# Decode holds, tiny steps on GpSimd and a later bias in a fused attention and two-expert-layer kernel

## The chip, the cores and the metric

The kernel runs on one core of one Trainium2 chip, as one launch. The metric is the device time of that launch in microseconds (us); lower is better. The core has TensorE (PE in the profile, its weight loads PEld), VectorE (DVE), ScalarE (ACT), GpSimd (POOL) and SyncE (SP), each with an instruction queue of its own that it works off in order, and DMA queues. TensorE's clock has two levels here, 1.2 and 2.4 GHz; the profile gives it as 0.5 and 1.0 of full speed.

## The reference

Three layers, all in float32, on 2304 tokens (4 sequences of 576) of width 512:

```python
scores = scale * q @ k^T, a causal window of 64, softmax        # 8 heads of 64
x = attention @ v                                               # 2304 x 512
h = x @ w_in;  g = softplus(h);  x = g @ w_out                  # 512 -> 2048 -> 512
logits = x @ w_gate + modality_bias[modality_id]                # 8 experts
out = p_best * (relu(x @ w1[e]) @ w2[e]),  e = argmax(logits)   # 512 -> 1024 -> 512
```

## The kernel before, in words

The kernel works in float32 accuracy out of reduced-precision matmuls: every matrix is split into a high part and the rest, and three matmuls (high by high, high by rest, rest by high) make one product.

The tokens of the first two layers are cut into 6 blocks of 384. Attention goes in chunks of 64 queries (c = 0 to 35, six to a block): `a_scores` makes the scores on TensorE, takes each row's maximum on VectorE (L143), scales it by -1/8 (L144, a 128x4 tile) and takes four exponentials on ScalarE (L148), which also give the row sums; `a_norm` adds 1e-9 to the sums (L153, 128x4), inverts them (L154) and multiplies (L159 on VectorE for the first block, L157 on ScalarE for the second, L159 on GpSimd from the third on); `a_probs` transposes the probabilities on TensorE (L165) and copies them out of PSUM on ScalarE (L167, tile pT); `a_av` multiplies by v (L180) and splits the result into xh (ScalarE, L181) and xl (VectorE, L88 called from L182). A block of the next layer can begin once xh and xl of its six chunks are there. "First-block attention" below means chunks 0 to 5, which run at the start; chunks 6 to 11 run beside the first block of the second layer, spread over its steps by `attn_slots`.

The second layer is 16 steps f of 128 hidden columns for each block b: `mm1(b, f)` is 12 matmuls (L238 to L240) into a PSUM tile ph, of which there are two, then softplus on ScalarE and VectorE (the "gate": L245, L246, L250 and L254 on ScalarE, L251 and the difference gl of L255 on VectorE; from the second block on L248 takes L245's place and gl is made on GpSimd); `mm2(b, f)`, two steps later, is 9 matmuls (L267 to L269).

The weights of step f, both of w_in and w_out, come from memory as 64-bit floats and are decoded in the kernel once, by `w_decode(f)`, during the start and the first block: ScalarE takes the absolute value (L222), VectorE does two clamping and shifting steps (L223, L224) and two merging steps (L225, L226), ScalarE rounds the high part (L227), VectorE takes the rest (L88 called from L228). For f in `HALVES` = (0, 1, 2) this goes in two halves of 512 columns, for the others in one pass of 1024. The decoded weights W0 to W15 stay on the chip, and the five later blocks use them again. The program calls `w_decode(0)` and `w_decode(1)` inside the loop over the first six chunks (L721), and `w_decode(f + 2)` in step f of the first block (L747).

`r_consts` (L305, called in step 2 of the first block) loads the small constants of the third layer and forms the bias of each token, `btok`, by five VectorE instructions (L316 to L321). `btok` is first read by `r_pick(0)`, in step 5 of the second block. The third layer starts after the sixth block with gathered tokens.

The order of an engine's instructions isn't written by hand: a planner walks the program with its own estimate of times and lets each engine take the earliest instruction of the program that it holds to be ready. So VectorE's queue can have a decode instruction ahead of an attention instruction that comes earlier in the program. `wait_for` (L202) adds a wait on another instruction, which the planner also respects. On the chip the order is then fixed.

Of the kernel before, what the change touches and what calls it, by code (L numbers as in the profile page):

```python
# [19 lines left out]
P = 128  # L20
# [14 lines left out]
def attention_moe_moe_kernel(ctx, tc, q, k, v, w_in, w_out, modality, w_gate, mod_bias, w1, w2, out):  # L35
# [17 lines left out]
    TPB = TB // P  # L53
    SCALE = 1.0 / 8.0
    LAG = 2
    HALVES = (0, 1, 2)
    BUSY = 2 * CPB
    R = N + P
    MR = 4
# [28 lines left out]
        eng.tensor_tensor(out_, a, hi.bitcast(F32), ALU.subtract)  # L88

    at = {}  # L90
    xblk = {}


# [22 lines left out]
    def a_scores(c, tags=None, s=None):  # L116
        w = at[c]
        win, n, qT, kT = w["win"], w["n"], w["q"], w["k"]
        if tags is None:
            both = ps.tile([P, 2, 4, P], F32, name="pss", tag="pS")  # L120
            parts = [both[:, :, 0:2, 0:n]]
            bank = [both[:, z, 0:2, 0:n] for z in range(2)]
        else:
            bank = [ps.tile([P, 2, P], F32, name=f"pss{z}", tag=tags[0], bufs=tags[1])[:, :, 0:n] for z in range(2)]
            parts = [x[:, None] for x in bank]
        for i in range(2):
            heads = [(2 * i + e, z) for e in range(2) for z in range(2)]
            outs = [bank[z][half(j, z) * C:(half(j, z) + 1) * C, i, :] for j, z in heads]
            for (j, z), o in zip(heads, outs):
                r = slice(z * C, (z + 1) * C)  # L130
                nc.tensor.matmul(o, qT[r, j, :], kT[r, :, j, :], start=True, stop=c >= BUSY)
            if c < BUSY:
                for (j, z), o in zip(heads, outs):
                    r = slice(z * C, (z + 1) * C)
                    nc.tensor.matmul(o, identb[r, r], mask[r, win], start=False, stop=True)
        s = sb.tile([P, 2, 2, P], F32, name="s") if s is None else s
        if c >= BUSY:
            nc.vector.tensor_tensor(s[:, :, :, 0:n], parts[0], mask[:, None, None, win].to_broadcast((P, 2, 2, n)), ALU.add)
            parts = [s[:, :, :, 0:n]]
            bank = [s[:, z, :, 0:n] for z in range(2)]  # L140
        mx = sb.tile([P, 2, 2], F32, name="mx")
        for i, x in enumerate(parts):
            nc.vector.tensor_reduce(out=mx[:, i:i + x.shape[1]], in_=x, axis=AX.X, op=ALU.max)  # L143
        nc.vector.tensor_scalar(mx, mx, -SCALE, None, ALU.mult)  # L144
        sm = sb.tile([P, NPR], F32, name="sm")
        for z in range(2):
            for i in range(2):
                nc.scalar.activation(s[:, z, i, 0:n], bank[z][:, i, :], AF.Exp, bias=mx[:, z, i:i + 1], scale=SCALE, accum_out=sm[:, 2 * z + i:2 * z + i + 1])  # L148
        w.update(s=s.rearrange("p z i k -> p (z i) k"), sm=sm)

    def a_norm(c):
        s, sm, n = at[c]["s"], at[c].pop("sm"), at[c]["n"]
        nc.vector.tensor_scalar(sm, sm, 1e-9, None, ALU.add)  # L153
        nc.vector.reciprocal(sm, sm)  # L154
        if CPB <= c < BUSY:
            for i in range(NPR):
                nc.scalar.activation(s[:, i, 0:n], s[:, i, 0:n], AF.Copy, scale=sm[:, i:i + 1])  # L157
        else:
            (nc.vector if c < CPB else nc.gpsimd).tensor_tensor(s[:, :, 0:n], s[:, :, 0:n], sm[:, :, None].to_broadcast((P, NPR, n)), ALU.mult)  # L159

    def a_probs(c, tag="pA", bufs=1, pT=None):
        s, n = at[c].pop("s"), at[c]["n"]
        pp = ps.tile([P, NPR, P], F32, name="pp", tag=tag, bufs=bufs)
        for j in range(NPR):
            nc.tensor.transpose(pp[0:n, j, :], s[:, j, 0:n], ident)  # L165
        pT = sb.tile([P, NPR, P], F32, name="pT", bufs=1) if pT is None else pT
        nc.scalar.copy(pT[0:n], pp[0:n])  # L167
        at[c]["pT"] = pT

    def a_av(c, tag="pA"):  # L170
# [27 lines left out]

    W = {}
    raws = {}  # L200

    def wait_for(later, earlier, reason):  # L202
        tc.add_manual_dep(later.ins, earlier.ins.name, mybir.DependencyInfo(mybir.DependencyClass.Sync, mybir.DependencyReason.DATA), reason=reason)
# [10 lines left out]
    def w_decode(f):  # L214

        raw = raws.pop(f)
        w = wp.tile([P, 2, 2, 512], F32R, name=f"W{f}", tag="W")
        t = sb.tile([P, 2, 512], I32, name="wt", bufs=1)
        for h in ([slice(0, 1), slice(1, 2)] if f in HALVES else [slice(0, 2)]):
            hw, lw, th = raw[:, h, :, 1], raw[:, h, :, 0], t[:, h, :]  # L220
            tf, hf = th.bitcast(F32), hw.bitcast(F32)
            nc.scalar.activation(tf, hf, AF.Abs)  # L222
            nc.vector.tensor_scalar(tf, tf, LEAST, MOST, ALU.max, ALU.min)  # L223
            nc.vector.tensor_scalar(th, th, 3, 0x3FFFFFF8, ALU.logical_shift_left, ALU.bitwise_and)  # L224
            nc.vector.scalar_tensor_tensor(hw, hw, SIGN_EXP, th, ALU.bitwise_and, ALU.bitwise_or)  # L225
            nc.vector.scalar_tensor_tensor(hw, lw, 29, hw, ALU.logical_shift_right, ALU.bitwise_or)  # L226
            nc.scalar.copy(w[:, h, 0, :], hf)  # L227
            diff(nc.vector, w[:, h, 1, :], hf, w[:, h, 0, :])  # L228
        W[f] = w
# [75 lines left out]
    def r_consts():  # L305
        nc.sync.dma_start(wg, w_gate.rearrange("(k p) e -> p k e", p=P))
        nc.sync.dma_start(bias2, mod_bias.rearrange("m e -> (m e)")[None, :].to_broadcast((P, 2 * E)).rearrange("p (m e) -> p m e", m=2))
        nc.sync.dma_start(mraw, modality.bitcast(I32).rearrange("(t p two) -> p t two", p=P, two=2))

        scr = wp.tile([P, 2048], F32, name="scr0", tag="W")  # L310
        tini = scr[:, :E * R // P * MR].bitcast(I32).rearrange("p (r m) -> p r m", m=MR)
        nc.gpsimd.memset(tini, 0)
        nc.gpsimd.memset(tini[:, :, 0:1], 4 * N)
        nc.sync.dma_start(meta.rearrange("(p r) m -> p r m", p=P), tini)
        sel = scr[:, 1024:1024 + 2 * NT].rearrange("p (m t) -> p m t", m=2)
        nc.vector.tensor_scalar(sel[:, 0], mraw[:, :, 0], 0.0, None, ALU.is_equal)  # L316
        nc.vector.tensor_scalar(sel[:, 1], mraw[:, :, 0], 0.0, None, ALU.not_equal)
        b1 = scr[:, 1100:1100 + NT * E].rearrange("p (t e) -> p t e", e=E)
        for m_, o_ in ((0, btok), (1, b1)):
            nc.vector.tensor_tensor(o_, sel[:, m_, :, None].to_broadcast((P, NT, E)), bias2[:, m_:m_ + 1, :].to_broadcast((P, NT, E)), ALU.mult)  # L320
        nc.vector.tensor_tensor(btok, btok, b1, ALU.add)  # L321
# [411 lines left out]
    def run(slots, pos):  # L733
        for p_, fn, c in slots:
            if p_ == pos:
                fn(c)

    for g in range(steps + LAG):
# [8 lines left out]
                    w_decode(f + 2)  # L747
        if b == 0 and f == 2:
            r_consts()
        run(slots, 0)  # L750
        t0 = (b - 1) * TPB
        if b == 0 and f == NF - 2:
# [127 lines left out]
```

## Time and profile before

| | |
|---|---|
| median of 3 runs | 778.92 us (778.86 to 779.86) |
| the profiled execution's own time | 781.15 us |
| its span in the trace | 779.1 us |
| granted TensorE clock, mean over the span | 0.978 |
| TensorE matmul busy | 735.8 us, 94% |
| VectorE busy | 448.2 us, 58% |
| ScalarE busy | 361.6 us, 46% |
| GpSimd busy | 236.4 us, 30% |

The busy shares are means over stages that have different limits, and a busy TensorE is not TensorE at its peak, since matmuls overlap. So the page's line of 40 slices and the windows by stage say more than the totals. In a timeline row the columns are start, duration, engine, line, operation, output<-input, shape, count, and in brackets the idle time of the engine before it with what ended it. An instruction's own duration overlaps the next one's by some hundredths of a microsecond, so what it costs its engine is the distance to the next start.

### The profile page before, as it was taken

The numbers are of one execution on the slowest core, as the hardware profiler recorded it, in microseconds if no ns is written. First come the engines' busy times: TensorE is split into PE (matmuls) and PEld (weight loads), VectorE is DVE, ScalarE is ACT, GpSimd is POOL, SyncE is SP. The second block draws the span as 40 slices with busy tenths as digits, with TensorE's granted clock in tenths as the row PEclk, the third lists the DMA queues.
The fourth block names the chain that finished last, engine by engine and source line by source line (L and its number), as shares of the span: only waits on it lengthen the run. The fifth ranks groups of instructions, "written<-read, shape, count | busy, mean of one in ns | idle before, by whom it ended". The sixth has DMA issues, their size and how long they took to land. (4 is left out here: it accounts for less than half of the span.)

```text
span 779.1 us, 12784 instructions
## 1 busy us (share of the span) xinstructions
PE 735.8 (94%) x4527; PEld 617.7 (79%) x4527; DVE 448.2 (58%) x1049; ACT 361.6 (46%) x867; POOL 236.4 (30%) x268
## 2 busy tenths in 40 slices
PE   5669999999989999999999999999989999999995
PEld 4457788888878888888788889878778888888884
DVE  6999994894397336953794349753432322223243
ACT  5779875545454445455545434543122212222143
POOL 2000000234225222333234213551464344353311
PEclk9769999999999999999999999999999999999998
DMA  9866433301141112111411015042021111111100
GB/s 329 295 212 212 155 101 122 117 1 50 36 128 42 28 48 89 35 48 49 129 36 20 23 40 200 26 178 100 17 71 50 35 56 47 37 57 43 41 28 17
DMA packets 42266, 65.17 MB, mean 84 GB/s; under 512 B 12797, under 2 KB 25469, under 8 KB 42056
## 3 DMA queue, kind: packets, MB, share of 16 engines
q1 hardware_dynamic: 37656, 54.45, 21.4%
q0 software_dynamic: 4528, 9.74, 3.8%
q8 instruction: 37, 0.61, 0.3%
q14 instruction: 45, 0.37, 0.2%
HBM read 54.37 MB, written 10.06 MB: 83 GB/s over the span
## 5 line engine op out<-in xcount | busy, mean ns | idle before, releaser
L88 POOL TENSOR_TENSOR gl<-a,gh 128x384 fp32r<-128x384 f32 x80 | 89.3, 1117 | 176.6 <-ACT gh L254 112.2
L238 PE MATMUL ph<-xh,W 128*128 128x384 f32 x384 | 133.5, 350 | 7.6 <-DVE a L251 6.1
L239 PE MATMUL ph<-xl,W 128*128 128x384 f32 x384 | 131.3, 342 | 0.8 <-DVE xl L88 0.8
L240 PE MATMUL ph<-xh,W 128*128 128x384 f32 x384 | 131.0, 341 | 0.0
L267 PE MATMUL px<-W,gh 128*128 128x512 f32 x288 | 116.3, 404 | 0.0
L268 PE MATMUL px<-W,gh 128*128 128x512 f32 x288 | 114.9, 399 | 0.0
L269 PE MATMUL px<-W,gl 128*128 128x512 f32 x288 | 107.3, 401 | 0.8 <-POOL gl L88 0.8
L249 ACT ACTIVATE a<-a 128x384 f32<-128x384 f32 x80 | 42.0, 525 | 104.2 <-DVE a L248 104.1
L159 POOL TENSOR_TENSOR s<-s,sm 128x512 f32<-128x512 f32 (+1 forms) x24 | 26.0, 1082 | 199.3 <-DVE sm L154 173.9
L238 PEld LDWEIGHTS ph<-xh,W 128*128 128x128 f32 x384 | 72.7, 190 | 15.4 <-DVE a L251 8.1
L629 POOL DMA_INDIRECT gx<-x2s,pieces x76 | 73.6, 968 | 23.6 <-issue 14.0
L239 PEld LDWEIGHTS ph<-xl,W 128*128 128x128 f32 x384 | 72.8, 190 | 4.2 <-DVE xl L88 1.5
L248 DVE TENSOR_SCALAR a<-ph 128x384 int32<-128x384 int32 x80 | 44.1, 551 | 51.6 <-PE ph L240 48.8
L251 DVE SCALAR_TENSOR_TENSOR a<-ph,a 128x384 f32<-128x384 f32 x96 | 53.0, 552 | 35.7 <-ACT a L250 35.6
L240 PEld LDWEIGHTS ph<-xh,W 128*128 128x128 f32 x384 | 73.0, 190 | 0.2
L254 ACT CAST gh<-a 128x384 fp32r<-128x384 f32 x96 | 49.0, 512 | 47.3 <-DVE a L251 45.6
L269 PEld LDWEIGHTS px<-W,gl 128*128 128x128 f32 x288 | 53.1, 188 | 13.4 <-POOL gl L88 1.7
L658 PE MATMUL p<-w,x2h 128*128 128x512 f32 x152 | 62.3, 410 | 1.2 <-ACT x2h L644 1.2
L267 PEld LDWEIGHTS px<-W,gh 128*128 128x128 f32 x288 | 54.4, 189 | 10.7 <-issue 1.2
L268 PEld LDWEIGHTS px<-W,gh 128*128 128x128 f32 x288 | 54.5, 189 | 8.9 <-issue 0.3
L661 PE MATMUL p<-w,x2h 128*128 128x512 f32 x152 | 60.4, 397 | 0.0
L662 PE MATMUL p<-w,x2l 128*128 128x512 f32 x152 | 60.3, 398 | 0.0
(196 smaller groups left out, 1335.2 us busy)
## 6 DMA issues: line engine op xcount, KB each, us to landing
raw<-in_moe_w_in_dram SPq DMA_DIRECT2D x16, 512.0 KB
raw<-in_moe_w_out_dram SPq DMA_DIRECT2D x16, 512.0 KB
r<-in_moe_w_dram SPq DMA_DIRECT2D x8, 1024.0 KB
qk<-in_k_dram SPq DMA_DIRECT2D x27, 256.0 KB
vr<-in_v_dram SPq DMA_DIRECT2D x27, 256.0 KB
qk<-in_q_dram SPq DMA_DIRECT2D x30, 128.0 KB
x2s<-xr SPq DMA_DIRECT2D x15, 256.0 KB
early<-in_v_dram SPq DMA_DIRECT2D x5, 256.0 KB
```

What stands on the lines that cost most here:

```text
L88: eng.tensor_tensor(out_, a, hi.bitcast(F32), ALU.subtract)
L238: nc.tensor.matmul(ph, W[f][:, 0, 0, sl], xh[:, c, :], start=c == 0, stop=False)
L239: nc.tensor.matmul(ph, W[f][:, 0, 0, sl], xl[:, c, :], start=False, stop=False)
L240: nc.tensor.matmul(ph, W[f][:, 0, 1, sl], xh[:, c, :], start=False, stop=c == KD - 1)
L251: nc.vector.scalar_tensor_tensor(a, ph, 0.0, a, ALU.max, ALU.add)
L267: nc.tensor.matmul(px[b][t], gh[:, sl], W[f][:, 1, 0, :], start=f == 0, stop=False)
L268: nc.tensor.matmul(px[b][t], gh[:, sl], W[f][:, 1, 1, :], start=False, stop=False)
L269: step["mm2"] = nc.tensor.matmul(px[b][t], gl[:, sl], W[f][:, 1, 0, :], start=False, stop=f == NF - 1)
L629: g = nc.gpsimd.indirect_dma_start(out=xr[:, c].rearrange("p c d -> p (c d)"), out_offset=None, in_=x2s[0:rows, :].rearrange("n (r f) -> ( ...
L658: first = nc.tensor.matmul(p, ah(c), bh(c), start=c == 0, stop=False)
L661: nc.tensor.matmul(p, ah(c), bl(c), start=False, stop=False)
L662: nc.tensor.matmul(p, al(c), bh(c), start=False, stop=c == n - 1)
```

## The change

Four edits, all of them around the start:

- `HALVES` = (0,): W1 and W2 are decoded in one pass each instead of two halves.
- `marks[c]` remembers the copy of the transposed probabilities of chunk c (L167). `HOLD` = {1: 3, 2: 5, 3: 5, 4: 5}: the first decode instruction (the absolute value on ScalarE) of W1 waits for that copy of chunk 3, those of W2, W3 and W4 for that of chunk 5.
- For chunks 0 to 11 (`c < BUSY`) the two 128x4 instructions L144 and L153 run on GpSimd instead of VectorE.
- The five bias instructions leave `r_consts` for `r_bias`, with a scratch tile of its own, called in step 0 of the second block.

```diff
-    HALVES = (0, 1, 2)
+    HALVES = (0,)
...
+    marks = {}
...
-        nc.vector.tensor_scalar(mx, mx, -SCALE, None, ALU.mult)
+        (nc.gpsimd if c < BUSY else nc.vector).tensor_scalar(mx, mx, -SCALE, None, ALU.mult)
...
-        nc.vector.tensor_scalar(sm, sm, 1e-9, None, ALU.add)
+        (nc.gpsimd if c < BUSY else nc.vector).tensor_scalar(sm, sm, 1e-9, None, ALU.add)
...
-        nc.scalar.copy(pT[0:n], pp[0:n])
+        marks[c] = nc.scalar.copy(pT[0:n], pp[0:n])
...
+    HOLD = {1: 3, 2: 5, 3: 5, 4: 5}
...
-            nc.scalar.activation(tf, hf, AF.Abs)
+            d_ = nc.scalar.activation(tf, hf, AF.Abs)
+            if f in HOLD:
+                wait_for(d_, marks[HOLD[f]], 'attention first')
...
-        sel = scr[:, 1024:1024 + 2 * NT].rearrange("p (m t) -> p m t", m=2)
+
+    def r_bias():
+        tmp = sb.tile([P, (2 + E) * NT], F32, name="rb", bufs=1)
+        sel = tmp[:, :2 * NT].rearrange("p (m t) -> p m t", m=2)
         nc.vector.tensor_scalar(sel[:, 0], mraw[:, :, 0], 0.0, None, ALU.is_equal)
         nc.vector.tensor_scalar(sel[:, 1], mraw[:, :, 0], 0.0, None, ALU.not_equal)
-        b1 = scr[:, 1100:1100 + NT * E].rearrange("p (t e) -> p t e", e=E)
+        b1 = tmp[:, 2 * NT:].rearrange("p (t e) -> p t e", e=E)
...
+        if b == 1 and f == 0:
+            r_bias()
```

## Rows read from the trace of the kernel before

**Rows 1.** The page, parts 1 (busy time) and 2 (40 slices, VectorE)

```profile
PE 735.8 (94%) x4527; PEld 617.7 (79%) x4527; DVE 448.2 (58%) x1049; ACT 361.6 (46%) x867; POOL 236.4 (30%) x268
...
DVE  6999994894397336953794349753432322223243
```

**Rows 2.** Busy time by stretch: length, engines' busy us (instructions), TensorE clock, DMA

```profile
30.00:40.00 10.00, 5.65 (x64) 4.28 (x64) 9.95 (x20) 8.81 (x29) 0.00 (x0) 0.50 0.68 259
...
50.90:90.20 39.30, 36.36 (x272) 29.28 (x270) 37.96 (x59) 36.52 (x86) 0.00 (x0) 0.96 0.57 190
90.20:122.40 32.20, 32.20 (x199) 26.52 (x199) 27.32 (x43) 24.48 (x56) 1.04 (x1) 1.00 0.35 113
...
62.00:770.00 708.00, 696.67 (x4102) 586.55 (x4101) 393.42 (x934) 316.57 (x741) 229.64 (x235) 1.00 0.22 69
```

**Rows 3.** TensorE timeline: mm1 of steps 0, 2, 3 and 15, first block

```profile
46.59 0.69 PE L239 MATMUL ph<-xl,W 128*128 128x384 f32 x1
...
55.06 0.44 PE L238 MATMUL ph<-xh,W 128*128 128x384 f32 x1 [2.79 <-DVE a L251]
...
62.51 0.44 PE L238 MATMUL ph<-xh,W 128*128 128x384 f32 x1
...
127.10 0.45 PE L238 MATMUL ph<-xh,W 128*128 128x384 f32 x1
```

**Rows 4.** TensorE timeline: scores, product with v and transpose of early chunks

```profile
12.26 0.70 PE L131 MATMUL pss<-early,early 64*64 64x128 f32 x8 [0.80 <-PE pp L165]
...
14.42 1.10 PE L180 MATMUL pav<-pT,early 64*64 64x64 f32 x16
15.45 1.11 PE L165 MATMUL pp<-ident,s 128*128 128x128 f32 x4
```

**Rows 5.** VectorE timeline, 34 to 46 us: decode between the instructions of attention

```profile
34.78 0.17 DVE L154 RECIPROCAL sm<-sm 128x4 f32<-128x4 f32 x1
34.87 0.39 DVE L88 TENSOR_TENSOR xl<-pav,xh 128x256 fp32r<-128x256 f32 x1
...
36.31 0.68 DVE L159 TENSOR_TENSOR s<-s,sm 128x512 f32<-128x512 f32 x1
36.91 0.68 DVE L223 TENSOR_SCALAR wt<-wt 128x1024 f32<-128x1024 f32 x1
37.51 0.15 DVE L153 TENSOR_SCALAR sm<-sm 128x4 f32<-128x4 f32 x1
...
39.60 1.22 DVE L225 SCALAR_TENSOR_TENSOR raw<-raw,wt 128x1024 int32<-128x1024 int32 x1
40.73 0.42 DVE L88 TENSOR_TENSOR xl<-pav,xh 128x256 fp32r<-128x256 f32 x1
41.07 1.22 DVE L226 SCALAR_TENSOR_TENSOR raw<-raw 128x1024 int32<-128x1024 int32 x1
...
45.37 0.30 DVE L320 TENSOR_TENSOR btok<-scr,bias 128x144 f32<-128x144 f32 x1
45.58 0.30 DVE L320 TENSOR_TENSOR scr<-scr,bias 128x144 f32<-128x144 f32 x1
45.80 0.42 DVE L88 TENSOR_TENSOR xl<-pav,xh 128x256 fp32r<-128x256 f32 x1
```

**Rows 6.** VectorE timeline: the last decode instruction, of W15

```profile
121.24 1.23 DVE L88 TENSOR_TENSOR W<-raw,W 128x1024 fp32r<-128x1024 f32 x1 [2.33 <-ACT W L227]
```

**Rows 7.** VectorE timeline: the first instruction in the second block

```profile
138.06 0.69 DVE L356 SCALAR_TENSOR_TENSOR prod<-xr,wga 128x512 f32<-128x512 f32 x1 [4.61 <-ACT xr L367]
```

**Rows 8.** GpSimd and VectorE timelines: a small GpSimd instruction, and the two side by side

```profile
5.23 0.12 POOL L327 IOTA quarter<- 128x4 int32 x1
...
150.12 1.44 POOL L88 TENSOR_TENSOR gl<-a,gh 128x384 fp32r<-128x384 f32 x1 [2.19 <-ACT gh L254]
...
168.41 1.01 POOL L88 TENSOR_TENSOR gl<-a,gh 128x384 fp32r<-128x384 f32 x1 [2.41 <-ACT gh L254]
...
150.73 1.38 DVE L356 SCALAR_TENSOR_TENSOR prod<-xr,wga 128x512 f32<-128x512 f32 x1
```

## The prediction, made before the changed kernel was run

> **What bounds the kernel now.** I read the page first. TensorE has matmuls under way for 94% of the span, VectorE for 58%, but VectorE's line of slices begins with 9s and ends with 2s [rows 1]: the stages differ. The busy time by stretch shows where. From 62 to 770 us TensorE is busy for 696.67 of 708.00 us [rows 2]. What the start saves or loses there moves everything behind it by as much, and nothing later takes it up. At 30 to 40 us it is the other way round: VectorE 9.95 of 10, TensorE 5.65 and at a granted clock of 0.50 [rows 2]. The change lies in this start.
>
> The TensorE timeline gives its course. The first layer-two product that needs all of chunk 5 starts at 46.59; mm1 of step 2 starts at 55.06 after 2.79 us of waiting for a gate instruction of VectorE, step 3 at 62.51, step 15, the last one that needs a new weight, at 127.10 [rows 3]. The VectorE timeline shows why 46.59 is so late: the decode instructions L223, L225 and L226 stand between chunk 5's reciprocal (34.78), its normalization (36.31) and the xl of chunks 4 and 5 (40.73, 45.80) [rows 5]. VectorE works off decodes for steps that TensorE needs only after 55 us, and the attention that TensorE waits for queues behind them.
>
> So there are two clocks to watch: **T**, when first-block attention and W1 are done, and when **W15** is done, now at 121.24 plus some 1.13, thus 122.37 [rows 5, 6]. W15 is 4.7 us ahead of its use at 127.10. An earlier T gains no more than W15 lets through.
>
> **Part one: the holds, and T.** They take no work away. They keep W1 out of the queues until chunk 3 is transposed and W2 to W4 until chunk 5 is; all of W5 to W15 come behind those, since one work tile serves every decode. T is bounded below by TensorE at its slow pace: from 12.26 it has four chunks of scores (two chunks take 12.26 to 14.42, so 1.08 each), five transposes and six products with v of about 1.04 each [rows 4], 4.3 + 5.2 + 6.2 = 15.7, so 28.0, and xh and xl behind the last (two instructions of about 0.4 by the xl row [rows 5]) make 28.8. Above, nothing better than today's 46.2 is certain. I take 34.8: to 28.8 I add one full decode, W1's, which falls into the middle (two instructions of 0.60 and three of 1.13 [rows 5], 4.6 us), and 1.4 us for the four new hops to GpSimd in chunks 4 and 5, 0.35 each, three times the 0.12 of the small GpSimd instruction [rows 8]. That is nearer to the lower end, because what lies between now and 46.2 is mostly decode.
>
> **Part two: VectorE's account at 34.8.** Before, VectorE has by then also done W2 and, of W3, the two clamping steps and the first merging one: 4.6 + 2 x 0.60 + 1.13 = 6.9 us that the changed kernel still owes; also chunk 6's maximum, 0.60 (as the normalization of as many elements). Against this, before still owes what the changed kernel has behind it: one reciprocal (0.09), one normalization (0.60), three xl (about 0.33 each), 1.7 us [rows 5]. Net 5.8 behind.
>
> **Part three: what is taken off VectorE.** The bias: three instructions of 0.21 or 0.22 [rows 5] and two small ones at about the 0.09 of the reciprocal, 0.8 us. In the second block they fall into the 4.61 us in which VectorE waits for ScalarE ahead of its first instruction there [rows 7]; without that cover they would cost 0.8 us of VectorE, off TensorE's path. The tiny steps still ahead at 34.8: eleven (one of chunk 6, two each of 7 to 11) at 0.09, 1.0 us. The one-pass decode of W1 and W2 only drops the fixed part of five instructions per step, under 0.4 us each and already in the 4.6. Now 5.8 - 0.8 - 1.0 = 4.0 behind: with the idle time of before, W15 would be done at 126.4.
>
> **Part four: the idle time.** From 50.9 to 90.2 VectorE idles for 39.30 - 37.96 = 1.34 us, 3.4%; from 90.2 to 122.4 for 32.20 - 27.32 = 4.88, 15% [rows 2]. In that second stretch TensorE is full, and VectorE's instructions wait for ScalarE (W15's last one 2.33 us [rows 6]), which has gates to do that TensorE paces. With T early TensorE is the one that waits, so I give the second stretch the first one's rate: 1.1 us, 3.8 saved, W15 at 122.6. The bounds are 3.8 saved and none.
>
> **Part five: what GpSimd costs VectorE.** A small GpSimd instruction in this stretch has no row in which VectorE runs beside it. The nearest rows are larger: the difference gl takes 1.01 us alone and 1.44 beside VectorE's products, and such a product starting at 150.73, while gl runs, takes 1.38 [rows 8]: the two exclude each other. Bounds per step: below, nothing, since GpSimd is idle in this stretch and VectorE may be waiting anyway; above, half of a merging step of 1.22 spent waiting by GpSimd, with VectorE stuck behind it, 0.61. I take 0.05, half of the 0.12 that such an instruction lasts, as VectorE alternates with ScalarE work: twelve steps, 0.6 us. A gain beyond part three is excluded, as the 0.09 is counted there.
>
> **Sum.** W15 at 123.2, mm1 of step 15 at 123.3 instead of 127.10: 3.8 us earlier. TensorE's own work doesn't forbid it: even with the 15.9 us that steps 0 to 2 took at half-speed spells (46.59 to 62.51) and the 64.6 from step 3 to 15 [rows 3], it would reach step 15 at 34.9 + 80.5 = 115.4, and the 8 us between also cover further spells at a clock of 0.5. Loading hides: the DMA engines are under 60% busy from 50.9 on [rows 2], and the holds only delay the readers. The profiled execution took 781.15 us, its span 779.1 and 2.05 around it, which stays; 781.15 - 3.8 = 777.35. It lies 2.23 above the median of the runs, so the median to expect is 778.92 - 3.8 = 775.1.
>
> **The rivals.** *The idle stays* (parts one to three right, four wrong): VectorE and ScalarE still wait for each other at the end, since ScalarE is at 36.52 of 39.30 in the good stretch too [rows 2]. W15 at 127.0, gain zero: 778.9.
>
> *More than that*: W1 fits into gaps that attention leaves, T is 30, and the hops cost nothing: 4.8 + 0.6 more, 769.7. For it speaks that TensorE alone would allow 28.8.
>
> *T comes late*: the attention chain itself, scores, maximum, exponentials, transposes at a clock of 0.50, was the limit, and the holds leave VectorE idle for nothing. Each microsecond of T costs one; from T = 40.2 on it is slower by over 0.2%, and at 42 it gives 782.3. Against it: the decode instructions between chunk 5's steps [rows 5].
>
> *GpSimd in the chain* (slower): the reciprocal L154 stands in VectorE's queue behind a sum that GpSimd has not yet made because VectorE's own merging steps shut it out. At 0.61 a hop, twelve hops and two on chunk 5's chain are 8.5 us in place of 0.6: 783.0; it decides from about 0.45 a hop. The Trainium skill states this as a rule (SBUF — State Buffer, "Who interferes with whom"): a VectorE instruction with two SBUF inputs and a GpSimd one that reads SBUF take turns, each whole. The trace agrees for the large pair, 1.38 against 1.44 [rows 8]; no row shows it for a tiny one.
>
> That the change doesn't do what it says would be a planner that orders as before; the waits forbid it for W2 to W4.
>
> **How the numbers follow.** The forecast has 0.56, the idle rival 0.18, more 0.10, T late 0.08, GpSimd 0.08. A measurement of this kernel tells about 0.2% (1.6 us) from none. Faster is 0.56 + 0.10 = 0.66, same 0.18, slower 0.16. The likeliest case's own range, T two microseconds either way, at the one end with GpSimd costing nothing (0.6) and at the other with 0.5 less idle time saved, is 772.5 to 777.6. The range to hold 8 in 10 leaves out the far half of "more" and the far part of the two slower cases: 770.3 to 780.3.
>
> **What would show it.** Right: no decode instruction between chunk 5's steps; T near 35, mm1 of step 0 right behind; TensorE with waits of about a microsecond a step for W until step 15 at 123; VectorE idle before 35 and at 3 to 4% from there to W15; the bias inside VectorE's first wait of the second block. Wrong: T above 39; VectorE idle by 10% or more between 50 and 122; reciprocals L154 that wait for GpSimd; or long stretches at a clock of 0.5 behind 60 us, which I cost at nothing.

## The result, and the profile after

The changed kernel took 785.87 us (median; 784.32 to 786.71) against 779.39 (778.86 to 781.27) for the kernel before beside it: ratio 1.0076, 95% interval 1.0052 to 1.0101. Forecast were 775.1 and "faster"; it is slower, and outside the range. The profiled execution took 784.32 us with a span of 782.4, 3.3 us longer than the span before. So the two traces show only half of the 6.5 us between the medians: the profiled execution of after took the least time of its four, that of before (781.15) more than three of its four.

The page of the kernel after, parts 1 and 2, which answer to [rows 1], hardly differ:

```profile
PE 735.3 (94%) x4527; PEld 617.3 (79%) x4527; DVE 446.7 (57%) x1015; ACT 360.2 (46%) x863; POOL 248.1 (32%) x292
...
DVE  5699998884397335954595339852532322223242
```

The busy time by stretch of the kernel after shows more. Columns as in [rows 2]; the cuts are at the first block's last xl and at the last decode.

```profile
5.40:42.10 36.70, 22.92 (x290) 17.79 (x290) 25.36 (x54) 21.67 (x79) 5.54 (x17) 0.70 0.79 269
...
42.50:132.40 89.90, 83.56 (x611) 66.83 (x610) 86.88 (x127) 77.32 (x184) 10.39 (x14) 0.97 0.57 191
...
62.00:770.00 708.00, 688.38 (x4038) 579.29 (x4030) 402.25 (x936) 316.99 (x728) 232.24 (x238) 1.00 0.22 71
```

The first two stretches in the kernel before, cut at its own last xl and last decode:

```profile
5.40:46.20 40.80, 24.53 (x310) 18.62 (x314) 39.85 (x93) 29.96 (x97) 1.35 (x4) 0.78 0.90 313
...
46.20:122.40 76.20, 73.26 (x497) 60.22 (x490) 69.85 (x110) 64.45 (x147) 1.04 (x1) 0.96 0.48 158
```

VectorE now idles for 36.70 - 25.36 = 11.3 us before the attention's end (1.0 before), and for only 89.90 - 86.88 = 3.0 us from there to the last decode (6.4 of 76.2 before). And TensorE, which the prediction took to be nearly full from 62 to 770, is idle for 19.6 us there in place of 11.3 [rows 2]. On its timeline 4.7 of them lie between 108 and 132 us, where it now waits mostly for the last weights and else for ScalarE's gh, and 4.9 (2.2 before) between 214 and 228.

VectorE's timeline after, answering to [rows 5] and [rows 6]: the first attention block, and the last decode.

```profile
27.51 0.18 DVE L323 TENSOR_SCALAR rb<-mraw 128x18 f32<-128x18 int32 x1 [0.94 <-DMA mraw<-in_moe_modality_id_dram]
...
31.30 1.23 DVE L229 SCALAR_TENSOR_TENSOR raw<-raw,wt 128x1024 int32<-128x1024 int32 x1
...
33.05 1.22 DVE L230 SCALAR_TENSOR_TENSOR raw<-raw 128x1024 int32<-128x1024 int32 x1
35.13 0.42 DVE L88 TENSOR_TENSOR xl<-pav,xh 128x256 fp32r<-128x256 f32 x1 [0.87 <-ACT xh L182]
36.98 0.18 DVE L155 RECIPROCAL sm<-sm 128x4 f32<-128x4 f32 x1 [1.43 <-POOL sm L154]
37.68 1.22 DVE L88 TENSOR_TENSOR W<-raw,W 128x1024 fp32r<-128x1024 f32 x1 [0.52 <-ACT W L231]
...
39.42 0.42 DVE L88 TENSOR_TENSOR xl<-pav,xh 128x256 fp32r<-128x256 f32 x1
...
40.96 1.22 DVE L229 SCALAR_TENSOR_TENSOR raw<-raw,wt 128x1024 int32<-128x1024 int32 x1
42.09 0.42 DVE L88 TENSOR_TENSOR xl<-pav,xh 128x256 fp32r<-128x256 f32 x1
...
131.19 1.23 DVE L88 TENSOR_TENSOR W<-raw,W 128x1024 fp32r<-128x1024 f32 x1 [0.98 <-ACT W L231]
```

T is 42.5, not 34.8: decodes still stand between the last xl steps, and now there are waits too. The token biases (L323) are not in the second block, but at 27.5 us, waiting for their transfer. W15 is done at 132.4, not 123.2.

TensorE's timeline after: mm1 of steps 0 and 15 ([rows 3]), then the passage from the second block to the third.

```profile
41.49 1.01 PE L242 MATMUL ph<-xh,W 128*128 128x384 f32 x2 [0.47 <-ACT xh L182]
...
131.41 0.34 PE L242 MATMUL ph<-xh,W 128*128 128x384 f32 x1
...
216.01 0.66 PE L166 MATMUL pp<-ident,s 128*128 128x128 f32 x4 [1.72 <-DVE xl L88]
...
219.02 1.01 PE L242 MATMUL ph<-xh,W 128*128 128x384 f32 x2
...
227.49 0.44 PE L242 MATMUL ph<-xh,W 128*128 128x384 f32 x1 [2.43 <-DVE a L255]
...
230.81 0.63 PE L271 MATMUL px<-W,gh 128*128 128x512 f32 x1
```

To see where time comes and goes, I take the start of mm2 of each step, counted through the blocks (16 steps each), less the same start before. The **lead** is 5.1 us at step 0, gone at step 12, 1.5 at step 18 and 1.6 at step 30, the last but one of the second block. At step 32, the first of the third (230.81 after, 227.25 before), it has become a **lag** of 3.6; at the end of layer two it is 4.4, and 1.6 us come back at the start of layer three. So the waits for late weights ate up the first block's lead, but they made the second block no later than before: it began 1.5 us earlier. The loss arose more than 100 us behind the last changed instruction, a tiny step of chunk 11, whose xl comes at 103.0. VectorE's timeline there, first before, then after (one row of the products, L356 and L363, in between is shown):

```profile
220.57 0.69 DVE L356 SCALAR_TENSOR_TENSOR prod<-xr,wgc 128x512 f32<-128x512 f32 x1
...
221.50 0.56 DVE L248 TENSOR_SCALAR a<-ph 128x384 int32<-128x384 int32 x1
...
223.91 0.55 DVE L251 SCALAR_TENSOR_TENSOR a<-ph,a 128x384 f32<-128x384 f32 x1
```

```profile
220.81 0.69 DVE L363 SCALAR_TENSOR_TENSOR prod<-xr,wgc 128x512 f32<-128x512 f32 x1
...
223.74 1.40 DVE L363 SCALAR_TENSOR_TENSOR prod<-xr,wga 128x512 f32<-128x512 f32 x1
225.08 0.08 DVE L363 DVE_READ_ACCUMULATOR prod<-xr,wga 128x1 f32 x1
225.08 0.55 DVE L252 TENSOR_SCALAR a<-ph 128x384 int32<-128x384 int32 x1
...
226.88 0.55 DVE L255 SCALAR_TENSOR_TENSOR a<-ph,a 128x384 f32<-128x384 f32 x1
```

Before, the eight products of one token tile precede the sign step (L248) of the block's first group, and the gate (L251) ends at 224.5. After, twelve precede it (L252), and the gate (L255) ends at 227.4; mm1 of step 2 and mm2 of step 0 wait. No line of the change touches this. VectorE's order is the planner's, and four products more stand in front. That the planner moved them because of other costs at the start is my reading: the traces show the order and not its reason.

### The profile page after: what moved, and what is told of

It reads as the page before. It is cut to its first block, busy times and chain, and to the rows that moved or that the text cites. A ratio compares the mean times of both kernels' runs of the same rounds, so it can differ in the third digit from the quotient of the medians.

```text
span 782.4 us, 12774 instructions
## 1 busy us (share of the span) xinstructions
PE 735.3 (94%) x4527; PEld 617.3 (79%) x4527; DVE 446.7 (57%) x1015; ACT 360.2 (46%) x863; POOL 248.1 (32%) x292
## 5 line engine op out<-in xcount | busy, mean ns | idle before, releaser
L243 PE MATMUL ph<-xl,W 128*128 128x384 f32 x384 | 132.1, 344 | 0.5 <-DVE xl L88 0.4
L273 PE MATMUL px<-W,gl 128*128 128x512 f32 x288 | 104.9, 401 | 0.8 <-POOL gl L88 0.7
L252 DVE TENSOR_SCALAR a<-ph 128x384 int32<-128x384 int32 x80 | 44.2, 552 | 51.7 <-PE ph L244 49.0
L255 DVE SCALAR_TENSOR_TENSOR a<-ph,a 128x384 f32<-128x384 f32 x96 | 53.1, 553 | 35.4 <-ACT a L254 35.4
L273 PEld LDWEIGHTS px<-W,gl 128*128 128x128 f32 x288 | 53.1, 188 | 13.2 <-POOL gl L88 1.6
L272 PEld LDWEIGHTS px<-W,gh 128*128 128x128 f32 x288 | 54.5, 189 | 8.9 <-issue 0.3
```

The source lines that it names most:

```text
L243: nc.tensor.matmul(ph, W[f][:, 0, 0, sl], xl[:, c, :], start=False, stop=False)
L255: nc.vector.scalar_tensor_tensor(a, ph, 0.0, a, ALU.max, ALU.add)
L272: nc.tensor.matmul(px[b][t], gh[:, sl], W[f][:, 1, 1, :], start=False, stop=False)
L273: step["mm2"] = nc.tensor.matmul(px[b][t], gl[:, sl], W[f][:, 1, 0, :], start=False, stop=f == NF - 1)
```

## The experiments

The runs were made on four chips. Each ratio is to the kernel before on the same chip. On three of the chips every profiled kernel takes 7 to 9 us more at one place of layer three (571 to 576 us before), so I compare ratios, and leads only up to the end of layer two. T below is the end of the first block's last xl; "lead" is against the one trace of before, negative for a lag. How far a lead can be trusted: after, s_again and s_order, whose orders are alike up to the third block, give 1.0 to 1.5 us at step 18, while p_bias and u_bias3, with one order up to there, differ by 2.3 us on two chips. So leads on different chips that differ by under some 2 us say little.

**The four parts alone.** Each is its hunks of the diff, applied to the kernel before.

> The holds alone, added to the kernel before. If the holds starve VectorE at the start (theory of the holds): first-block attention done near 40 us, VectorE idle some 8 us before it, W15 near 130, and the steps up to the second block's end no earlier than before; the run about 3 us or more slower. If the GpSimd steps are what kept attention late (theory of the hop): without them attention is done near 35, W15 near 123, and the run is about 4 us faster. If most of the loss is made at the passage from the second to the third block (theory of the passage), where the planner's order decides: whatever the start does, the sign of the whole is that of the wait of TensorE around 210 to 230 us, 5 us with it and nothing without.

> The 24 tiny steps on GpSimd alone, added to the kernel before. Theory of the hop: the GpSimd steps that meet a merging step last 1 us instead of 0.23, ScalarE waits for them, attention is done later than 46.2 us and the run is 3 us or more slower. Theory of the holds: within 1.5 us of before. Theory of the passage: the start moves by under 2 us, and the whole moves by more only if the wait at 210 to 230 us changes.

> W1 and W2 in one pass alone, added to the kernel before. Theories of the holds and of the hop: within 1 us of before. Theory of the passage: within 1 us up to 205 us, and then 0 or some 5 us by the wait at 210 to 230 us.

> The bias in its own function alone, added to the kernel before. In the changed kernel the planner still ran it at 27.5 us; if it does so here too, VectorE waits up to 1 us for its data in the start and the run is within 1 us of before up to 205 us by all theories; by that of the passage it then has 0 or some 5 us more.

| run | ratio (interval) | T | W15 | lead at steps 18, 30, 32, end of layer two |
|---|---|---|---|---|
| p_hold | 1.0023 (1.0009 to 1.0038) | 42.0 | 129.5 | 0.1, 0.1, -3.5, -3.2 |
| p_tiny | 1.0064 (1.0033 to 1.0095) | 51.5 | 121.6 | 0.5, 0.6, -2.5, -4.5 |
| p_halves | 1.0097 (1.0072 to 1.0123) | 54.8 | 118.8 | -6.6, -7.0, -7.1, -7.2 |
| p_bias | 0.9994 (0.9978 to 1.0010) | 44.6 | 120.8 | 3.9, 3.4, 3.3, 0.9 |

The parts alone add up to 1.8%, the whole costs 0.76: they are not separate costs. p_hold has T and W15 as the theory of the holds said, but its loss lies at the passage; p_tiny is 5.0 us slower, as the theory of the hop said; p_halves, which no theory expected beyond 1 us up to 205 us, has lost 6.6 us by step 18 and hardly any behind it. Each part alters the planner's order, in two ways. Tiny steps on GpSimd, or whole decodes, let decodes get ahead of the attention (T 51.5 and 54.8 against 46.2): W15 comes sooner, TensorE starts later. And the passages differ: p_hold and p_tiny lose 3.6 and 3.1 us between steps 30 and 32, where the whole change loses 5.2, p_bias none there, but 5.4 between steps 46 and 48, ahead of the fourth block, of which 2.5 come back by step 62.

**All products behind gates.** To take the order out of the comparison, in every block:

```
-        nc.vector.scalar_tensor_tensor(a, ph, 0.0, a, ALU.max, ALU.add)
+        gate[b, f] = nc.vector.scalar_tensor_tensor(a, ph, 0.0, a, ALU.max, ALU.add)
...
-            nc.vector.scalar_tensor_tensor(out=prod, ...
+            d_ = nc.vector.scalar_tensor_tensor(out=prod, ...
+            if e == 0:
+                wait_for(d_, gate[b + 1, i], 'gate first')
```

q_pass is this on the kernel after, q_bpass on the kernel before; q_pass_vec is q_pass with the two tiny steps on VectorE; q_pass_xl is q_pass with the marks on the last subtraction of the attention and W1's decode behind it:

```
-        diff(nc.vector, xl[:, :, col], po, xh[:, :, col])
+        marks[c] = diff(nc.vector, xl[:, :, col], po, xh[:, :, col])
...
-    HOLD = {1: 3, 2: 5, 3: 5, 4: 5}
+    HOLD = {1: 5, 2: 5, 3: 5, 4: 5}
```

> The kernel after, with one thing added: the first product of each token tile (the long VectorE product of the router) waits for VectorE's gate instruction of the same block's step with the tile's number, so that the products no longer stand ahead of the first gates of a block. Theory 'passage': the loss of the kernel after arises where the second block passes to the third (six steps there took 38.4 us in the kernel before, 42.9 after), because the planner put nine products ahead of the first gate; the order now is the same whatever the start was. The six steps fall to below 36 us, the time falls by at least 5 us against the kernel after, to 0.990 to 0.998 of the kernel before. Rival 'start': the late last decode (132.4 us against 122.5) is what costs the time; the passage only shows it; then the time stays within 1.5 us of the kernel after, 1.006 to 1.010 of the kernel before.

> The kernel before, with the same waits of products for gates and nothing of the change. Theory 'passage': passages of both kernels are now alike, so only the start tells them apart; at step 18 of layer two the kernel after led by 1.5 us, so this run is 0.5 to 3 us slower than q_pass, and 2 to 10 us faster than the kernel before (its own six steps there took 38.4, 33.2, 35.8 and 29.6 us in the four passages; 29.6 is what a passage takes without a wait). Rival 'start': this run is 4 to 7 us faster than q_pass, as the kernel before is faster than the kernel after.

> q_pass with the tiny steps back on VectorE (the other parts of the change stay). Theory 'passage' by itself: the tiny steps on GpSimd cost what VectorE and ScalarE waited for them in the start; with c0 to c5 chained through them the first block's attention ended 5.3 us later in the run of that part alone, so here it ends 1 to 5 us earlier than in q_pass, and the time falls by 0 to 3 us. Rival 'the tiny steps are the loss': the time falls by 4 us or more against q_pass. Rival 'VectorE is relieved by them': the time rises by 1 us or more.

> q_pass with the waits set two steps further on: decodes of weight steps 1 to 4 wait for VectorE's last subtraction of the sixth chunk (xl) in place of ScalarE's copy of its transposed probabilities, and step 1's decode is written behind the first block's attention. Theory 'marker': in the kernel after, the mark was passed at 35 us while two chunks' products and subtractions still stood behind the decode of step 1 in VectorE's queue, which is why the first block's attention ended at 42 us and not at 34.8; here it ends at 33 to 37 us, and TensorE's first product of layer two starts 5 to 8 us earlier. Rival 'chain': the attention of the first block is a chain through ScalarE, GpSimd and TensorE that ends at 40 us or later whatever VectorE decodes. For the time: if an earlier start is worth nothing since the decoded weights come no sooner (the last decode stays at 130 us or later), the time is within 1.5 us of q_pass; if the earlier start counts, it falls by 3 to 6 us.

| run | ratio (interval) | T | W15 | lead at steps 18, 30, 32, 46, end of layer two |
|---|---|---|---|---|
| q_pass | 1.0211 (1.0177 to 1.0245) | 42.2 | 132.1 | 1.8, 1.8, 1.4, 2.4, -13.7 |
| q_bpass | 1.0181 (1.0141 to 1.0222) | 46.8 | 122.3 | 0.2, -0.8, -1.3, -0.2, -13.2 |
| q_pass_vec | 1.0274 (1.0231 to 1.0316) | 46.0 | 137.1 | -4.7, -4.7, -7.2, -9.0, -21.8 |
| q_pass_xl | 1.0354 (1.0321 to 1.0387) | 39.5 | 139.9 | -6.0, -5.9, -10.7, -9.7, -22.5 |

The times of q_pass, q_bpass and q_pass_xl are far from all that was expected; q_pass_vec is 6.1 us slower than q_pass, as its rival 'VectorE is relieved by them' said. In the second passage q_pass kept its lead (1.8 to 1.4, then 2.4), so the order there is confirmed as that loss. But with a wait in every block the two kernels come out 2.1 and 1.8% above the kernel before. The products held back then stand where the next block's attention should: the last product of the third block starts at 251.4 us in q_pass and 241.3 before, the xl of chunk 19 comes at 261.6 and 253.2, that of chunk 23, the last of the fourth block, at 302.3 and 295.5, and mm1 of the fourth block waits for chunk 23 (302.3 against 298.4). So a wait that helps at one passage costs at the next.

q_pass_xl tells two things. T falls by 2.7 us only, with every held decode out of the way. And the earlier start is worth nothing: W15 comes 7.8 us later than in q_pass, and so does step 18 (160.8 against 153.0 us).

**Four products at one passage.** The wait now holds in the third block alone, for the second token tile's first product, behind the sign step:

```
-            nc.vector.tensor_scalar(a.bitcast(I32), ph.bitcast(I32), SIGN, None, ALU.bitwise_or)
+            first[b, f] = nc.vector.tensor_scalar(a.bitcast(I32), ph.bitcast(I32), SIGN, None, ALU.bitwise_or)
...
+            d_ = nc.vector.scalar_tensor_tensor(out=prod, ...
+            if b + 1 in (2,) and (i, e) == (1, 0):
+                wait_for(d_, first[b + 1, 0], 'gate first')
```

s_order is this on the kernel after; s_vec and s_split put the tiny steps back on VectorE, or HALVES = (0, 1, 2) back; s_again is the kernel after itself.

> The kernel after with one wait: in the third block alone, the first product of the second token tile waits for VectorE's first instruction on the result of the block's first product group (the sign step of step 0). The planned order of VectorE then differs from that of the kernel after in four products alone, which move behind that instruction; from the fourth block on the two orders are alike. Theory 'order at the passage': in the kernel after, twelve products stand ahead of that instruction and eight in the kernel before, and this is what turned a lead of 1.5 us into a lag of 4.3; the six steps of the passage fall from 42.9 to 38 to 40 us, and the time by 3 to 5 us, to 0.997 to 1.003 of the kernel before. Rival 'start': the late last decode costs the time, the wait at the passage would only move: within 1 us of the kernel after, 1.006 to 1.010.

> The kernel after once more, beside the three others on one chip: 1.005 to 1.010 of the kernel before, and the six steps of the second passage at 42 to 44 us if that wait belongs to the kernel's order and not to one execution; if it was an accident of that execution, 38 to 40 us and 1.000 to 1.004.

> s_order with the tiny steps back on VectorE; from the third block on its planned order of VectorE is the same as that of s_order, so a difference arises in the start. From the pair of runs with all passages held (808.1 against 800.5 us of span) the tiny steps on GpSimd gain up to 7 us beside the waits of decodes, though alone they cost 5 us. Theory 'relief': 3 to 8 us slower than s_order. Rival 'hop' (what VectorE and ScalarE waited for GpSimd, 8.0 and 10.9 us in the first 62 us, is a net loss): 1 us or more faster.

> s_order with the decodes of steps 1 and 2 in halves again, as in the kernel before; planned order from the third block on as in s_order. Theory 'chain' (whole decodes of 2.3 us a step stand in VectorE's queue ahead of the attention of the first block, and halves let TensorE start step 1 sooner; alone, whole decodes cost 7.6 us): 1 to 4 us faster than s_order. Rival 'supply' (what counts is how soon the last decode is done, and halves cost VectorE 0.2 to 0.4 us a step): 0 to 1 us slower.

| run | ratio (interval) | T | W15 | lead at steps 18, 30, 32, end of layer two |
|---|---|---|---|---|
| s_again | 1.0063 (1.0041 to 1.0084) | 43.0 | 133.0 | 1.0, 1.0, -3.0, -3.4 |
| s_order | 1.0012 (1.0002 to 1.0023) | 42.6 | 132.5 | 1.4, 1.5, -0.4, -0.7 |
| s_vec | 1.0126 (1.0103 to 1.0150) | 45.2 | 136.3 | -3.9, -3.9, -7.0, -8.8 |
| s_split | 1.0020 (1.0006 to 1.0034) | 43.0 | 132.5 | 1.4, 1.5, -0.4, -0.8 |

Moving four products takes 3.6 us off the median (784.56 to 780.98), and the intervals don't touch. The six steps from step 30 on take 39.2 us in s_order and 41.3 in s_again (38.4 before, 42.9 after). VectorE's timeline of s_order at the passage:

```profile
220.89 0.69 DVE L365 SCALAR_TENSOR_TENSOR prod<-xr,wgc 128x512 f32<-128x512 f32 x1
...
222.85 0.56 DVE L254 TENSOR_SCALAR a<-ph 128x384 int32<-128x384 int32 x1 [0.48 <-PE ph L246]
223.44 0.69 DVE L365 SCALAR_TENSOR_TENSOR prod<-xr,wga 128x512 f32<-128x512 f32 x1
...
224.80 0.55 DVE L257 SCALAR_TENSOR_TENSOR a<-ph,a 128x384 f32<-128x384 f32 x1
```

The sign step now waits for TensorE, not behind products, and the gate ends 2.1 us sooner than after. The start is as after, W15 at 132.5 included, so the rival "start" is out as the cause of these 3.6 us. What remains is a kernel that is even with the one before, not better.

s_vec shows what the tiny steps on GpSimd are worth here. The busy time of s_order and s_vec between T and W15:

```profile
42.60:132.50 89.90, 83.48 (x611) 66.75 (x610) 86.89 (x127) 77.31 (x184) 10.37 (x14) 0.97 0.57 191
```

```profile
45.20:136.30 91.10, 83.64 (x598) 68.91 (x590) 83.29 (x131) 74.26 (x174) 3.38 (x3) 0.95 0.53 180
```

VectorE idles 3.0 us in the one and 7.8 in the other, but that only says where its idle time lies: from 5.4 us to W15 it idles 14.5 and 15.0 us. What differs is its work up to W15, 112.61 us in s_order and 115.97 in s_vec: the 24 tiny steps cost it 3.4 us, 0.14 each, and W15 comes 3.8 us later. With the holds in place, GpSimd's tiny steps gain 1.1% (8.9 us, a little more than the theory of the relief had), though alone they cost 0.6%. Halves or whole decodes make no difference that shows under the holds.

**The rest of the set, and the end of the attention.** u_nohold is s_order without HOLD, u_nobias s_order with the biases in the scratch tile again. u_chain has the late marks of q_pass_xl and the tiny steps on VectorE, without a wait at the passage. u_bias3 is p_bias with the first product of the fourth block behind its sign step.

> s_order without the waits of decodes 1 to 4 for the first attention block (tiny steps on GpSimd, whole decodes and the biases' place stay). Theory 'parts hang together': each of the two parts alone cost 5.0 and 7.6 us, because decodes get ahead of the attention and TensorE starts late; without the waits that comes back: first product of layer two at 48 us or later and 4 to 10 us slower than s_order. Rival 'waits cost': the late decodes are the loss, the last decode comes at 120 to 124 us and the run is 1 to 3 us faster than s_order.

> s_order with the token biases formed where the kernel before forms them (in the shared scratch tile). In the kernel after they stand at 28 us in VectorE's queue, not in the second block. Theory 'nothing hangs on them' (0.8 us of work, and 0.94 us of waiting for their transfer): within 1.5 us of s_order. Rival 'the wait in the chain counts': biases later, first attention block earlier by 1 us or more, and 1.5 to 4 us faster.

> The kernel after with all decodes of steps 1 to 4 behind the last subtraction of the first attention block, as in q_pass_xl (attention done at 39.1 us there), and the tiny steps on VectorE. Theory 'hop': VectorE waited 6.0 us for GpSimd in that stretch, so the attention ends at 33 to 36 us, as the prediction had it (34.8). Rival 'chain of the other engines' (GpSimd itself waited 8.4 us for ScalarE's exponentials): it ends at 37.5 to 39.5 us, whoever does the tiny steps.

> The kernel before with the biases' part alone, as in p_bias, and one wait: in the fourth block the first product waits for VectorE's sign step of step 0. In p_bias layer two led the kernel before by 3.4 us until step 46 and lost 5.4 us at the passage to the fourth block, where four products stood ahead of that step and three behind it ahead of the gate. Theory 'order at the passage': that loss goes, and the time is 2 to 5 us below the kernel before, ratio 0.993 to 0.998. Rival 'the loss moves on' (the later blocks' order is planned anew and loses it there): 0.998 to 1.003.

Then two runs with the exponentials of the second block's first chunk held: v_chain6 is u_chain with it, v_c6 is s_order with it.

```
-                nc.scalar.activation(s[:, z, i, 0:n], bank[z][:, i, :], AF.Exp, ...
+                e_ = nc.scalar.activation(s[:, z, i, 0:n], bank[z][:, i, :], AF.Exp, ...
+                if c == CPB and z + i == 0:
+                    wait_for(e_, ends[CPB - 1], 'first block first')
```

(ends[c] is the chunk's xl, as marks[c] in u_chain.)

> u_chain with one wait more: the exponentials of chunk 6, the first of the second block, wait for the last subtraction of the first block. Theory 'next block in the queue': chunk 6 and 7's exponentials and scalings take about 5.6 us of ScalarE between 31 and 39 us in u_chain; without them the first block's attention ends at 33 to 36.5 us. Rival 'the chain itself' (transposes, products and their PSUM buffers at a clock of 0.50): it ends at 38 us or later.

> s_order with the same wait for chunk 6 (the decode of step 1 stays in the middle of the attention, the tiny steps on GpSimd). Theory 'next block in the queue': the first block's attention ends at 36 to 39 us in place of 42.2, VectorE idles 2 us or more less before that, and the time falls by 1 to 4 us against s_order, to 0.996 to 1.000 of the kernel before. Rival 'account' (VectorE's and ScalarE's work on the second block is only put off, and is due by 135 us all the same): the end of the attention moves, the time stays within 1 us of s_order.

| run | ratio (interval) | T | W15 | lead at steps 18, 30, 32, end of layer two |
|---|---|---|---|---|
| u_nohold | 1.0133 (1.0105 to 1.0162) | 54.5 | 121.2 | -4.2, -6.7, -9.4, -9.6 |
| u_nobias | 1.0036 (1.0022 to 1.0051) | 41.9 | 132.3 | 1.7, 1.7, -1.2, -1.6 |
| u_bias3 | 1.0019 (0.9999 to 1.0040) | 45.1 | 122.8 | 1.6, 1.1, 1.1, -2.2 |
| u_chain | timed once: 799.39 us | 39.6 | 138.7 | -4.7, -4.7, -7.8, -9.8 |
| v_chain6 | timed once: 793.46 us | 37.2 | 136.8 | -3.0, -2.9, -6.3, -5.9 |
| v_c6 | 1.0014 (0.9996 to 1.0032) | 40.1 | 131.1 | 2.8, 2.9, -1.1, -1.4 |

Without the holds the other parts cost 1.3%: T is 54.5, as the theory had it (first product at 52.1). Where the biases stand matters little: with them in the scratch tile again T is 41.9 in place of 42.6, and the time 0.24% above that of s_order, on another chip and with intervals that just touch, so their new place costs nothing that shows. u_bias3's rival came true: it loses 2.6 us in place of 5.4 ahead of the fourth block and 1.4 more ahead of the fifth, where p_bias lost nothing; and its lead at step 18 is 1.6, not 3.9, though VectorE's planned order up to there is the same. Executions on two chips can differ by that much.

T is the same with the tiny steps on VectorE (39.6) as on GpSimd (39.5), so the hop isn't the limit. ScalarE's timeline of u_chain shows what stands between chunks 3, 4 and 5 (an xh each at 32.81, 36.06 and 38.83):

```profile
31.43 0.37 ACT L149 ACTIVATE s<-pss,mx 128x128 f32<-128x128 f32 x1 [2.87 <-DVE mx L145]
...
33.54 1.30 ACT L158 ACTIVATE s<-s,sm 128x128 f32<-128x128 f32 x4
35.36 0.37 ACT L149 ACTIVATE s<-pss,mx 128x128 f32<-128x128 f32 x1 [0.52 <-DVE mx L145]
...
37.65 1.28 ACT L158 ACTIVATE s<-s,sm 128x128 f32<-128x128 f32 x4 [0.51 <-DVE sm L155]
38.83 0.35 ACT L182 CAST xh<-pav 128x256 fp32r<-128x256 f32 x1
```

L158 runs for chunks of the second block only: the softmax of chunks 6 and 7 is threaded into the first block's end. With it held, v_chain6's last chunks follow at 2.05 us each (VectorE's timeline):

```profile
32.71 0.42 DVE L88 TENSOR_TENSOR xl<-pav,xh 128x256 fp32r<-128x256 f32 x1 [1.60 <-ACT xh L184]
34.76 0.42 DVE L88 TENSOR_TENSOR xl<-pav,xh 128x256 fp32r<-128x256 f32 x1 [1.63 <-ACT xh L184]
36.81 0.42 DVE L88 TENSOR_TENSOR xl<-pav,xh 128x256 fp32r<-128x256 f32 x1 [1.63 <-ACT xh L184]
```

T is 37.2, between the two expectations, with 2.90 us of VectorE waiting for the biases' transfer ahead of it in this run. v_c6 beside s_order gives as much, 2.5 us.

v_c6 brings T to 40.1 and a lead of 2.9 at step 30, twice that of s_order. All of it is gone at step 32, and in time its rival came true. TensorE's timeline there, first before, then v_c6:

```profile
211.41 0.69 PE L180 MATMUL pav<-pT,vr 128*64 128x64 f32 x16
...
214.26 0.40 PE L269 MATMUL px<-W,gl 128*128 128x512 f32 x1
...
215.19 0.66 PE L165 MATMUL pp<-ident,s 128*128 128x128 f32 x4
```

```profile
211.68 0.69 PE L184 MATMUL pav<-pT,vr 128*64 128x64 f32 x16
...
214.69 0.66 PE L169 MATMUL pp<-ident,s 128*128 128x128 f32 x4 [1.72 <-DVE xl L88]
...
218.19 1.01 PE L247 MATMUL ph<-xh,W 128*128 128x384 f32 x2
...
219.98 0.53 PE L248 MATMUL ph<-xl,W 128*128 128x384 f32 x1
```

TensorE's own order differs too. Before, nine instructions of the second block's last mm2 (212.30 to 214.26) stand behind chunk 16's product with v and cover the time until that chunk's xl, and chunk 17's transposes start without a wait. In v_c6, as in after and s_order, that product stands behind the last mm2, and TensorE waits 1.72 us for the xl and 0.73 for the copy of chunk 17. So the third block's first product starts at 218.19, as against 219.02 after and 218.13 before, though the second block was ahead; and an instruction of it takes 0.53 us, where full speed is 0.34. The four moved products don't touch this, and no run moves TensorE's order: what it costs is not measured.

## Why the prediction was wrong, point by point

**The premise failed.** "What the start saves or loses there moves everything behind it by as much, and nothing later takes it up", read from TensorE's 696.67 of 708.00. Passages between blocks take it up: at the second one the lead of after went from 1.6 us to a lag of 3.6, that of s_order from 1.5 to a lag of 0.4, that of v_c6 from 2.9 to a lag of 1.1. And the change lost time far from its own lines: an order that differs 100 us later cost 3.6 us (s_order beside s_again). The rest of the miss lies ahead of the passage: 3.8 us were forecast, and the lead at step 18 is 1.5. What was to be seen in that row was its 11.3 us of idle time: 2.2 of them lie at the second passage, where TensorE waits for VectorE and for the last chunk of attention, and a TensorE that is busy elsewhere is no proof that it couldn't wait longer.

**Part one, T = 34.8, was 42.5.** The lower bound counted the first block's chunks alone. The planner threads the second block's softmax through ScalarE at the same time (v_chain6: 2.4 us of T), W1's decode stands in front of the last xl steps (q_pass_xl: 2.7), and the biases wait for their transfer in VectorE's queue (0.94). The marks are at fault too: they sit at the transpose's copy, and two chunks' products and xl steps come behind it. "T late" gave this case 0.08 and its mechanism, the holds that leave VectorE idle, was there: 11.3 us idle. Its price wasn't: "each microsecond of T costs one" would have made the start some 4 us late at T = 42.5, and it was 1.5 us early at step 18. That its 782.3 for T = 42 lies nearer to the result than the forecast is luck.

**The sum's gauge, W15, was the wrong one.** It came at 132.4, not 123.2, yet the second block began no later: VectorE had done the second block's attention ahead of the decodes (the xl of chunk 11 at 103.0, before 133.0). From 5.4 us to W15 VectorE works 112.66 us (109.78 before) and idles 14.4 (7.3 before), and these are the 10.0 us by which W15 is later. So the account of parts two and three left out the idle time ahead of T, 11.3 us. As I read it, decodes and attention are both owed by the block's end, so their sum counts, not the last of one of them; no run separates the two. In q_pass_xl, where W15 came at 139.9, step 18 was 6.0 us late.

**Part four had the rate right, and it wasn't enough.** The idle time between T and W15 fell from 6.4 of 76.2 us to 3.0 of 89.9, 3.4%, the rate that I took. The 3.3 us saved there stand against 10.4 more ahead of T.

**Part five was too low for the step, and part three for the gain.** GpSimd's timeline after:

```profile
28.57 0.23 POOL L154 TENSOR_SCALAR sm<-sm 128x4 f32<-128x4 f32 x1 [1.62 <-ACT s L149]
33.28 1.06 POOL L145 TENSOR_SCALAR mx<-mx 128x4 f32<-128x4 f32 x1 [4.49 <-DVE mx L144]
...
41.20 1.06 POOL L145 TENSOR_SCALAR mx<-mx 128x4 f32<-128x4 f32 x1 [4.25 <-DVE mx L144]
```

A tiny step takes 0.23 us alone and 1.06 beside a merging step, until 34.34 and 42.26, just behind the ends of the merging steps (33.05 + 1.22 and 40.96 + 1.22). That is the lock that the Trainium skill states (SBUF — State Buffer, "Who interferes with whom"), and the trace agrees for the tiny step that no row of before could show. Beside a merging step a tiny step is thus 0.83 us longer, above the upper bound of 0.61, and VectorE waited 8.0 us for GpSimd in the first 62 us. Still the steps pay for themselves beside the holds: a tiny step on VectorE costs it 0.14 us (s_vec), not 0.09.

**The bias** isn't where the change says: the planner took its instructions when it could, at 27.5 us. "That the change doesn't do what it says" I had looked at for the holds alone. Its price is small (u_nobias).

Two things stay open. The traces show 3.2 us of the 6.5 between the medians; the rest differs from one execution to the next. And 1.6 us at the start of layer three come back in after and s_order, but not in u_nobias or s_vec; no run was made for that.

## What to carry to other kernels

Where a planner fixes the order of each engine's queue, a change at the start also reorders queues far behind it: compare the orders at every passage between blocks before believing a sum made for the start. Four products moved at one passage were worth 3.6 us here, nearly the whole forecast gain; a wait for gates in every block cost the kernel before 1.8%. A part that alone costs 0.6% can gain 1.1% once another is in place (the tiny steps beside the holds), and one that alone costs 1.0% can then cost nothing (the whole decodes), so leave one out of the whole as well as trying each alone.

## What the runs showed that I had not expected

The column of the granted clock can't be taken alone at the start. From 20 to 39.2 us it reads 0.50 after and 1.00 in v_chain6. v_chain6's stretch, and two groups of its TensorE timeline:

```profile
20.00:39.20 19.20, 15.06 (x141) 11.79 (x142) 8.31 (x26) 8.84 (x31) 0.00 (x0) 1.00 0.43 123
...
35.24 1.12 PE L183 MATMUL pav<-early 128*64 128x64 f32 x16 [0.93 <-DVE xl L88]
...
39.06 0.52 PE L244 MATMUL ph<-xh,W 128*128 128x384 f32 x1
```

The product with v takes 1.12 us there, as after (39.90, at 0.50), and 0.69 at 211.41 before, where the clock is 1.00; an instruction of mm1 takes 0.52, not 0.34. So by its rows the attention of v_chain6 ran at the lower of the two levels, whatever the column says. Before, from 10 to 20 us, it is the same: the column says 1.00, and the transposes take 1.11 us [rows 4], as against 0.66 at 215.19. At the second passage column and rows agree: from 212 to 231 us the clock is 1.00 before, 0.84 after and 0.82 in v_c6, whose 0.53 us in place of 0.34 take back a part of what an earlier start brings.
